# An attention scan and two mixtures of experts on one core: decay rows on ACT's DMA queue, two of eleven weight slots filled at the beginning, and another order of the last two attention steps, the tail and the preparation of w2

## The chip, the cores and the metric

The kernel runs on one core of a Trainium2 chip. The metric is the device time of one execution in microseconds (us), as the median of several runs. One further execution was recorded by the hardware profiler; all rows below come from it. The engines are named PE (TensorE matmul), PEld (its weight loads), DVE (VectorE), ACT (ScalarE), POOL (GpSimd) and SP (SyncE), and L352 is line 352 of the kernel.

## The reference

Three stages follow each other. The first is a gated linear attention over 4 batches, 8 heads, 768 positions and head size 40; the second a soft mixture of 8 experts with 4 slots each; the third a mixture whose weights are balanced over 8 rounds (Sinkhorn) and in which every expert sees all 3072 rows.

```python
# attention, per batch and head, t = 0..767
m_new  = max(f[t] + m, i[t])
C      = exp(f[t] + m - m_new) * C + exp(i[t] - m_new) * outer(v[t], k[t])
n      = exp(f[t] + m - m_new) * n + exp(i[t] - m_new) * k[t]
y[t]   = sigmoid(o[t]) * (C @ q[t]) / max(abs(n @ q[t]), 1)
# x: y as 3072 rows of 320
# first mixture (moe)
logits = x @ phi
d      = softmax(logits, over rows);   slot_in = d.T @ x
slot_out[e] = relu(slot_in[e] @ w1[e]) @ w2[e]
x      = softmax(logits, over slots) @ slot_out
# second mixture (moe2)
P = exp(x @ w_gate - max)
for _ in range(8): P /= P.sum(1) ; P /= P.sum(0) ; P *= N / E
out = sum over e of P[:, e] * (relu(x @ w1[e]) @ w2[e])
```

## The kernel before, in words

**Attention** is worked off in 24 tiles of 128 positions (all 8 heads of one batch, six tiles per batch). Keys and queries of a tile come in as kq (load_kq, L145, two loads of 160 KB made of 160-byte runs), values as vz (load_v, L150), the output gate as xr (load_o, L155). The gates are prepared once at the beginning (gates, L215 to L264): the running sum of the log decays is split into three bf16 parts, gp3, stored to DRAM as gpd (L250, L253), and read back per tile as three rows of the operand R (load_R, L308), the other 96 rows of which are a pattern of ones; its partner csl holds the input gates and is completed by small copies (load_csl, L275). One product of csl and R gives the exponents of a tile (e_p, L370, two halves per tile), ACT takes their exp into dd (L379), POOL cuts the triangle (L384), DVE multiplies in the scores q k (s_d, L407), and PE forms the value product from dd and vz (pv, L438); p_st (L448) adds the state of the earlier tiles. y_d (L459 to L476) and y_g (L486) normalise the tile into xr. x_p transposes finished tiles (L497), lg_p computes the logits (L520), lt_p, lt_d, lt_a and lt_f make the combine weights ct_all, and sl_p with sl_d (L592, L603) sum the dispatched rows into sacc.

**Order.** A step i of the loop mixes parts of several tiles; the string ORDER gives the sequence in which they are written, and PE, ACT and SP execute in that written order (manual schedules), while DVE and POOL are ordered by a scheduler. In step i, load_R fetches the decay rows of tile i + 3, needed by the exponent products of step i + 1; load_v fetches tile i + 2; load_kq tile i + 4; load_o tile i + 4; W fetches weights. All loads go over SP's queue. Ahead of the loop stands a prologue in which PE runs filler products (warm, WARM = [14, 10, 2, 2]).

**Weights.** The first mixture (MoE1) has 16 matrices of 1.28 MB, w1 and w2 of 8 experts. They go into slots (function slot): NRA = 9 slots exist while attention runs (wa, big, bigx, bigy) and are filled by parts, four per w1 and two per w2, WN[i] parts in step i; NRB = 6 further slots (wb) lie where attention's tiles were. Slot 14 takes w2 of MoE2's first expert, and freed slots are filled again.

**Tail.** After the loop, the string TAIL orders what is left: x22p, x22a, x23p, x23a are the transposes of the last two tiles and their copies; lp, ld, la, tp, tv and sp, sd the logits and the sums of the last group of four tiles; 0p to 4p with 0a and 0d transpose the combine weights of five of the six groups into cst (c_p, L787; c_a on ACT, L791; c_d on DVE, L795); ftp and ftd fold the sums into siT; wk is a pair of filler products (L872). Then MoE1 runs expert by expert (up, L910 and L917; up_t, L937; down, L948), the sixth group's c_p and the preparation of w2 of MoE2's first expert between them: amax takes the maxima, pow2_w a power-of-two scale, prep_a (ACT, L1023) and prep_d (DVE, L1027) split it into two f16 parts, wh and wl. Between MoE1 and MoE2 stand the fold of the slot outputs (L812), the router product (L1113), the first hidden weights of MoE2 (s1_p, s1_c) and the gate logits (gate_p, L1190).

**MoE2** takes 48 blocks of 512 rows: g1 (L1143) forms the hidden values z, ACT and DVE split them into hh and hl (L1146, L1147), and g2 multiplies them with wh and wl (L1164 to L1166).

Of the kernel before, what the change touches and what calls it, by code (L numbers as in the profile page):

```python
# [21 lines left out]
def mlstm_moe_kernel(  # L22
# [23 lines left out]
    P = 128  # L46
# [18 lines left out]
    ORDER = "LF' PK STm R DV DK O KT KTa ST STd E0 E0a E0g V I Y QT QTa Yg S W0 W1 E1 E1a E1g LP LV X Xa LD G LA W SM IR"  # L65
    PB = [1, 2, 3]
# [3 lines left out]
    NY = 2  # L70
    NRA = 2 + NBIG + NX + NY
    NRB = 6
# [105 lines left out]
    load_o(0, 1)  # L178

# [48 lines left out]
    def gates():  # L228
# [20 lines left out]

        nc.sync.dma_start(out=gpd[0:BH], in_=gp3[0:BH])  # L250
        load_R(0)
        load_R(1)
        nc.sync.dma_start(out=gpd[BH:GR], in_=gp3[BH:GR])  # L253
        load_kq(2)
        nc.scalar.copy(out=ident16, in_=ident)
        ids()
        init_R(0, 0, nc.scalar.copy)
        k_a(0, 0)
        k_a(0, 1)
        nc.scalar.activation(out=eG, in_=Gc, func=AF.Exp)  # L260
        nc.scalar.activation(out=eK, in_=eK, func=AF.Exp)
        for a, _ in zip((0, None, 1, None, 2), split3(cs3, bb, rk)):
            if a is not None:
                nc.gpsimd.tensor_copy(csl[a * BH:(a + 1) * BH, 0:SW], cs3[0:BH, a, :])  # L264
# [39 lines left out]
    def load_R(i):  # L304
# [3 lines left out]
        nc.sync.dma_start(out=t[96:99, :, :], in_=gpd[r0:r0 + H, :, o:o + L].rearrange("r a s -> a r s"))  # L308
# [318 lines left out]
    def slot(n):  # L627
# [10 lines left out]
        return rings["b"].tile([P, WSL], F32, tag="w", name="wb")  # L638
# [12 lines left out]
    def step(i):  # L651
# [6 lines left out]
        if gq < 0 or not X:  # L658
# [54 lines left out]
    load_v(1)  # L713
# [37 lines left out]
    WN = [0, 1, 1, 1] + [1 + (i % 6 > 3) for i in range(NT)]  # L751
# [3 lines left out]
    for i in range(NT + 1):  # L755
        step(i)
    if man2:
# [6 lines left out]
    rings["b"] = bctx.enter_context(tc.tile_pool(name="ring_b", bufs=NRB, side="right", reuse_waits="tile"))  # L764
# [3 lines left out]
    def load_n(n):  # L768

        if n < 2 * E - 2:  # L770
            load_w(m1_parts(n))
        elif n == 2 * E - 2:
# [26 lines left out]
    def c_m(g0, g1):  # L799
        nc.gpsimd.tensor_copy(cst[32:64, g0 * TB:g1 * TB], cst[0:32, g0 * TB:g1 * TB])  # L800
# [20 lines left out]
    cbk = [(ps_e, "e"), (ps_e, "e"), (ps_s, "s"), (ps_s, "s"), (ps_t, "t")]  # L821
# [52 lines left out]
    TAIL = "x22p x22a s4p wk 0p wk 1p x23p s4d 0a wk x23a lp wk 2p 1a 0d ld la mxp wk tp mxd ls lc 1d wk mbp mbd tv wk 3p mba fwd wk sp sd wk tq te wk ftp 4p ftd wk wk 2a 2d 3a 3d 4a ltd lta ltf 4d"  # L874
# [8 lines left out]
    for gq in range(gl):  # L883
# [11 lines left out]
    for gq in range(gl):  # L895
        c_m(gq, gq + 1)
# [45 lines left out]
    def down_p(e):  # L942
        hT = hTs.pop(e)
        w = m1[2 * e + 1].rearrange("p (k d) -> p k d", d=DM)
        pd = psy.tile([P, DM], F32, tag="y", name="pd")
# [96 lines left out]

    up(0)
    for e in range(E - 1):
        if e == 4:
# [8 lines left out]
        if e == 1:  # L1054
            c_p(gl, psp, "p")
            c_a(gl)
            c_d(gl)
            c_m(gl, NB)
        elif e == 4:
            src2[0] = w20[0].rearrange("p (k d) -> p k d", d=DM)  # L1060
# [293 lines left out]
```

## Time and profile before

| | us |
|---|---|
| median of 3 runs | 970.33 |
| lowest and highest run | 969.82 to 972.05 |
| the profiled execution, its own time | 971.88 |
| its span, first to last instruction | 969.6 |
| PE busy (7973 matmuls) | 939.5 |
| DVE busy | 569.1 |
| ACT busy | 357.3 |
| POOL busy | 88.2 |

The span is the time from the first to the last instruction of the profiled execution; its own time holds the launch around it too. A busy share is an average over stages that have different limits, and matmuls overlap in a pipeline, so PE's share says where PE was never idle rather than how fast it ran. Of 63.45 MB that DMA moved, most comes in the first 230 us: attention's inputs in short runs and the weights of MoE1.

### The profile page before, as it was taken

The numbers are of one execution on the slowest core, as the hardware profiler recorded it, in microseconds if no ns is written. First come the engines' busy times: TensorE is split into PE (matmuls) and PEld (weight loads), VectorE is DVE, ScalarE is ACT, GpSimd is POOL, SyncE is SP. The second block draws the span as 40 slices with busy tenths as digits, with TensorE's granted clock in tenths as the row PEclk, the third lists the DMA queues.
The fourth block names the chain that finished last, engine by engine and source line by source line (L and its number), as shares of the span: only waits on it lengthen the run. The fifth ranks groups of instructions, "written<-read, shape, count | busy, mean of one in ns | idle before, by whom it ended". The sixth has DMA issues, their size and how long they took to land.

```text
span 969.6 us, 18804 instructions
## 1 busy us (share of the span) xinstructions
PE 939.5 (97%) x7973; PEld 652.7 (67%) x7973; DVE 569.1 (59%) x1185; ACT 357.3 (37%) x696; POOL 88.2 (9%) x159
## 2 busy tenths in 40 slices
PE   6799999899999999999999999999999999999998
PEld 3687788535657766666666666666666666666665
DVE  6366466645778875474547456646755564554543
ACT  4254455334423334242434244224423342432321
POOL 4354344100000000000000000000000000000000
PEclk9799799999999999999999999999999999999999
DMA  6999999763020101010101011001100000000111
GB/s 95 159 179 191 183 192 233 266 213 120 15 85 12 40 15 55 1 55 1 55 1 55 1 55 28 30 1 55 55 1 1 1 1 1 1 2 28 48 41 48
DMA packets 129563, 63.45 MB, mean 65 GB/s; under 512 B 103528, under 2 KB 123272, under 8 KB 129480
## 3 DMA queue, kind: packets, MB, share of 16 engines
q1 hardware_dynamic: 129480, 62.26, 27.5%
q8 instruction: 62, 1.02, 0.5%
q14 instruction: 21, 0.17, 0.1%
HBM read 58.07 MB, written 4.08 MB: 64 GB/s over the span
## 4 chain that ended last, share of the span: by engine, by line
PE 93%; DVE 3%; ACT 1%; SPq 1%; DMA 1%; issue 1%; POOL 0%; DVEq 0%; ACTq 0%
PE y L1164 22%; PE y L1166 21%; PE y L1165 21%; PE z L1143 9%; PE oa L438 3%; PE ptk L352 2%; PE pss L400 2%; PE oa L448 2%; PE pu L910 2%; PE pe L370 2%; PE ob L412 1%; DMA R<-gpd 1%; PE pu L917 1%; PE pd L948 1%; PE ptx L497 1%; PE ob L285 1%
## 5 line engine op out<-in xcount | busy, mean ns | idle before, releaser
L1164 PE MATMUL y<-wx,hh 128*128 128x320 f16 x1344 | 403.8, 300 | 0.0
L1166 PE MATMUL y<-wx,hl 128*128 128x320 f16 x1344 | 401.9, 299 | 0.0
L1165 PE MATMUL y<-wx,hh 128*128 128x320 f16 x1344 | 401.9, 299 | 0.0
L1146 ACT ACTIVATE hh<-z 128x512 f16<-128x512 f32 x384 | 209.4, 594 | 452.4 <-PE z L1143 451.9
L1147 DVE SCALAR_TENSOR_TENSOR hl<-z,hh 128x512 f16<-128x512 f32 x384 | 248.3, 684 | 52.2 <-ACT hh L1146 51.6
L1179 DVE SCALAR_TENSOR_TENSOR acc<-y,Ps,acc 128x320 f32<-128x320 f32 x168 | 92.3, 549 | 218.3 <-PE y L1166 217.4
L1164 PEld LDWEIGHTS <-hh 128*128 128x128 f16 x1536 | 151.0, 98 | 100.8 <-issue 47.7
L1166 PEld LDWEIGHTS <-hl 128*128 128x128 f16 x1536 | 150.5, 98 | 61.1 <-DVE hl L1147 2.8
L1165 PEld LDWEIGHTS <-hh 128*128 128x128 f16 x1536 | 151.1, 98 | 51.4
L1143 PE MATMUL z<-cst,sst 96*128 96x512 f32 x384 | 142.0, 449 | 0.7 <-ACT gl L1198 0.4
L1143 PEld LDWEIGHTS z<-cst,sst 96*128 96x128 f32 x384 | 63.0, 191 | 11.1 <-issue 2.9
L1166 PE MATMUL y<-wh,hl 128*128 128x320 f16 x192 | 58.1, 303 | 0.8 <-DVE hl L1147 0.7
L1164 PE MATMUL y<-wh,hh 128*128 128x320 f16 x192 | 58.5, 304 | 0.0
L1165 PE MATMUL y<-wl,hh 128*128 128x320 f16 x192 | 58.1, 303 | 0.0
L360 ACT COPY T<-ptk 128x512 f32<-128x512 f32 x46 | 26.9, 586 | 41.5 <-PE ptk L352 41.5
L352 PE MATMUL ptk<-ident,kq 128*128 128x128 f32 x192 | 32.9, 301 | 8.5 <-POOL ident masks.py:199 8.5
L379 ACT ACTIVATE dd<-pe 128x512 f32<-128x512 f32 x48 | 29.0, 605 | 32.7 <-PE pe L370 31.8
L407 DVE TENSOR_TENSOR dd<-pss,dd 128x512 f32<-128x512 f32 x48 | 30.3, 671 | 7.1 <-PE pss L400 6.2
L459 DVE TENSOR_TENSOR u<-oa,eGt 128x164 f32<-128x164 f32 x20 | 6.6, 329 | 46.2 <-PE ob L448 46.2
L384 POOL TENSOR_SCALAR_AFFINE_SELECT dd<-dd 128x512 f32<-128x512 f32 x48 | 30.8, 641 | 25.9 <-ACT dd L379 25.4
L996 POOL PARTITION_ALL_REDUCE mr<-mxs x8 | 2.9, 368 | 309.8 <-DVE mxs L1015 309.8
L996 POOL PARTITION_ALL_REDUCE mr<-mx x8 | 3.0, 378 | 306.0 <-DVE mx L986 306.0
(230 smaller groups left out, 787.4 us busy)
## 6 DMA issues: line engine op xcount, KB each, us to landing
wa<-in_moe_w_dram SPq DMA_DIRECT2D x18, 512.0 KB, 6.0
raw<-in_moe_w_dram SPq DMA_DIRECT2D x28, 320.0 KB, 3.9
wb<-in_moe_w_dram SPq DMA_DIRECT2D x8, 640.0 KB, 7.8
kq<-in_k_dram SPq DMA_DIRECT2D x24, 160.0 KB, 4.9
kq<-in_q_dram SPq DMA_DIRECT2D x24, 160.0 KB, 5.2
vz<-in_v_dram SPq DMA_DIRECT2D x24, 160.0 KB, 4.3
xr<-in_o_gate_dram SPq DMA_DIRECT2D x24, 160.0 KB, 3.6
out_dram<-acc SPq DMA_DIRECT2D x24, 160.0 KB, 1.8
```

The costliest lines, as they stand in the source:

```text
L352: nc.tensor.transpose(pt[:, j, :], kq[i % NQ][:, a, 2 * j:2 * j + 2, :].rearrange("p h d -> p (h d)"), ident,)
L379: nc.scalar.activation(out=dd, in_=tmp.pop(("e", i, hh)), func=AF.Exp)
L384: nc.gpsimd.affine_select(out=dd, in_=dd, pattern=[[0, 4], [1, L]], compare_op=ALU.is_ge, fill=0.0, base=0, channel_multiplier=-1,)
L407: nc.vector.tensor_tensor(out=dds[i, r], in0=tmp["s", i][r], in1=dds[i, r], op=ALU.mult)
L438: nc.tensor.matmul(o_in[TH * a:TH * a + TH, 2 * j + r, :], dds[i, r][:, j, TH * a:TH * a + TH], vz[i % NV][:, 2 * j + r, :], start=True, s ...
L1143: nc.tensor.matmul(z, Sst[e][:, kc * P:(kc + 1) * P], cst[:, tb * TB:(tb + 1) * TB], start=True, stop=True,)
L1146: nc.scalar.activation(out=hh[:, kc, :], in_=z, func=AF.Relu)
L1147: nc.vector.scalar_tensor_tensor(out=hl[:, kc, :], in0=z, scalar=0.0, in1=hh[:, kc, :], op0=ALU.max, op1=ALU.subtract)
L1164: nc.tensor.matmul(y, hh[:, kc, ts], wh[e][:, kc, :], start=(kc == 0), stop=False)
L1165: nc.tensor.matmul(y, hh[:, kc, ts], wl[e][:, kc, :], start=False, stop=False)
L1166: nc.tensor.matmul(y, hl[:, kc, ts], wh[e][:, kc, :], start=False, stop=(kc == KF - 1))
L1179: nc.vector.scalar_tensor_tensor(out=a, in0=y, scalar=Ps[:, i, e:e + 1], in1=a, op0=ALU.mult, op1=ALU.add)
```

## The change

The change moves the stores of gpd, the loads of R and the copies of csl from SP's queue to ACT's; loads tile 2 of kq early; loads the first two weight matrices (one expert) in the prologue and gives bigy four slots instead of two and wb four instead of six, each with a name of its own; spreads the other weight parts one per step (WN), more in the last steps; orders DVE by hand in the last three steps, with another sequence (ORDER_L); writes the tail in another order, with three c_p in it instead of five and three wk instead of twelve; puts the other three c_p behind the first three experts; starts the maxima of w2 after experts 1 and 2 and converts one quarter after each of the experts 3 to 6; copies the combine rows (c_m) with one load on ACT's queue instead of six copies on POOL; computes s1_p ahead of the router product; and adds filler products (warm2) at the end of MoE1 and at the gate.

```diff
+    ORDER_L = "LF' PK STm R DV DK O ST STd V I S W0 W1 Y Yg LP LV X Xa LD G LA W"
-    NY = 2
+    NY = 4
-    NRB = 6
+    NRB = 4
     load_o(0, 1)
+    load_kq(2)
...
-        nc.sync.dma_start(out=gpd[0:BH], in_=gp3[0:BH])
-        load_R(0)
-        load_R(1)
-        nc.sync.dma_start(out=gpd[BH:GR], in_=gp3[BH:GR])
-        load_kq(2)
         nc.scalar.copy(out=ident16, in_=ident)
         ids()
         init_R(0, 0, nc.scalar.copy)
+        nc.scalar.dma_start(out=gpd[0:BH], in_=gp3[0:BH])
         k_a(0, 0)
-        k_a(0, 1)
         nc.scalar.activation(out=eG, in_=Gc, func=AF.Exp)
         nc.scalar.activation(out=eK, in_=eK, func=AF.Exp)
+        k_a(0, 1)
+        load_R(0)
+        load_R(1)
+        nc.scalar.dma_start(out=gpd[BH:GR], in_=gp3[BH:GR])
...
     def load_csl(g_):
-            nc.sync.dma_start(
+            nc.scalar.dma_start(
-    WARM = [14, 10, 2, 2]
+    WARM = [14, 3, 2, 2]
     def load_R(i):
-        nc.sync.dma_start(out=t[96:99, :, :], ...)
+        nc.scalar.dma_start(out=t[96:99, :, :], ...)
...
-            DV=lambda: T and load_v(n),
+            DV=lambda: T and i and load_v(n),
-        for o in ORDER.split():
+        for o in (ORDER if i < NT - 2 else ORDER_L).split():
...
-    load_v(1)
...
+    load_w(islice(ahead_parts, 2))
+    load_v(1)
+    load_v(2)
+    load_w(islice(ahead_parts, 2))
     load_o(1, O0)
+    load_w(islice(ahead_parts, 2))
     load_kq(3)
     load_csl(2)
-    load_w(islice(ahead_parts, 2))
...
-    WN = [0, 1, 1, 1] + [1 + (i % 6 > 3) for i in range(NT)]
+    WN = [0] + [1] * 19 + [2, 2, 2, 3, 0]
-    for i in range(NT + 1):
+    for i in range(NT - 2):
         step(i)
+    man2d = tc.manual_schedule(engines={mybir.EngineType.DVE})
+    man2d.__enter__()
+    for i in range(NT - 2, NT + 1):
+        step(i)
+    man2d.__exit__(None, None, None)
...
-    def c_m(g0, g1):
-        nc.gpsimd.tensor_copy(cst[32:64, g0 * TB:g1 * TB], cst[0:32, g0 * TB:g1 * TB])
+    def c_m():
+        nc.scalar.dma_start(out=cst[32:64, :].bitcast(F32), in_=cst[0:32, :].bitcast(F32))
-    cbk = [(ps_e, "e"), (ps_e, "e"), (ps_s, "s"), (ps_s, "s"), (ps_t, "t")]
+    cbk = [(ps_e, "e"), (ps_s, "s"), (ps_s, "s")]
-    TAIL = "x22p x22a s4p wk 0p wk 1p x23p s4d 0a wk x23a lp wk 2p 1a 0d ld la mxp wk tp mxd ls lc 1d wk mbp mbd tv wk 3p mba fwd wk sp sd wk tq te wk ftp 4p ftd wk wk 2a 2d 3a 3d 4a ltd lta ltf 4d"
+    TAIL = "x22p x22a 0p s4p 0a x23p x23a s4d 1p 2p lp 1a wk ld la mxp ls tp mxd wk tv mbp 0d mbd mba sp lc fwd sd wk tq ftp 1d te ftd 2a ltd lta ltf 2d"
...
     for e in range(E - 1):
-        if e == 4:
+        if e == 3:
             man4 = tc.manual_schedule(...)
...
-        if e == 1:
-            c_p(gl, psp, "p")
-            c_a(gl)
-            c_d(gl)
-            c_m(gl, NB)
-        elif e == 4:
-            for kk in range(4):
-                amax(0, kk)
-        elif e > 4:
-            if e == 5:
+        if e < 3:
+            c_p(3 + e, psp, "p")
+            c_a(3 + e)
+            c_d(3 + e)
+            if e:
+                for kk in range(2 * e - 2, 2 * e):
+                    amax(0, kk)
+        else:
+            if e == 3:
+                c_m()
                 pow2_w(0)
-            for kk in range(2 * e - 10, 2 * e - 8):
-                prep_a(0, kk)
-                prep_d(0, kk)
+            prep_a(0, e - 3)
+            prep_d(0, e - 3)
+    def warm2(n):
+        pw2 = psz.tile([P, TB], F32, tag="z", name="pw2").rearrange("p (a l) -> p a l", a=4)
+        for _ in range(n):
+            nc.tensor.matmul(pw2, ident16, ident16.unsqueeze(1).to_broadcast([P, 4, L]), start=True, stop=True)
     up_t(E - 1)
+    warm2(2)
     down_p(E - 1)
     down_d(E - 1)
+    warm2(4)
     fold_t(pt, soa, fold)
+    warm2(2)
+    s1_p(0)
+    pow2_s(0)
...
     gate_p(1)
+    s1_c(0, 0, True)
     gate_a(0)
-    s1_c(0, 0, True)
     gate_t(0)
+    warm2(2)
```

Three places show how the order changes. The first is SP's queue in the prologue, from the load of v of tile 1 on (wa are MoE1's first slots, kq_104 receives tile 3). Before:

```order
L150 DMA vz_111<-in_v_dram 128x8x40
L155 DMA xr<-in_o_gate_dram 128x8x40 x2
L145 DMA kq_104<-in_k_dram 128x8x40
L145 DMA kq_104<-in_q_dram 128x8x40
L275 DMA csl<-gbuf 32x256 x3
L622 DMA wa<-in_moe_w_dram 128x1024 x2
L155 DMA xr<-in_o_gate_dram 128x8x40 x2
L308 DMA R_122<-gpd 3x8x128
```

With the change, from the load of tile 2 on:

```order
L146 DMA kq_106<-in_k_dram 128x8x40
L146 DMA kq_106<-in_q_dram 128x8x40
L623 DMA wa<-in_moe_w_dram 128x1024 x2
L151 DMA vz_111<-in_v_dram 128x8x40
L151 DMA vz_112<-in_v_dram 128x8x40
L623 DMA wa<-in_moe_w_dram 64x512 x2
L156 DMA xr<-in_o_gate_dram 128x8x40 x2
L623 DMA wa<-in_moe_w_dram 128x4x320 x2
L146 DMA kq_104<-in_k_dram 128x8x40
L146 DMA kq_104<-in_q_dram 128x8x40
```

The loads of R and csl are gone from SP, six parts of the first two weight matrices stand ahead of the keys of tile 3, and v of tiles 1 and 2 comes early.

The second is ACT's queue with the change, from the end of the prologue into step 1, each row with what it waits for (DMAHW0 to DMAHW7 are eight counters that the DMAs take in turn; T are the copies of transposed keys and queries). Before, the same rows stood there without the two loads:

```order
L165 ACTIVATE xr<-xr 128x2x320 [waits DMAHW0_49]
L309 DMA R_122<-gpd 3x8x128 [waits DMAHW1_49]
L361 COPY T_349<-ptk 128x512 [waits PE_49,Activation_49]
L380 ACTIVATE dd<-pe 128x512 [waits PE_49]
L361 COPY T_391<-ptk 128x512 [waits PE_49]
L380 ACTIVATE dd<-pe 128x512 [waits PE_49]
L309 DMA R_121<-gpd 3x8x128 [waits DMAHW6_49]
L361 COPY T_424<-ptk 128x512 [waits DVE_49,PE_49]
```

R of tile 3 is issued ahead of step 0's first copy and R of tile 4 ahead of step 1's, each behind a wait for a counter.

The third is PE at the beginning of the tail (ptx are transposes of tiles, ptc those of the combine weights, pq is sl_p, pl the logits). The rows left out are the filler pairs. Before:

```order
L497 MATMUL ptx<-ident,xr 112x128 x6
L592 MATMUL pq<-xr,lt 32x321 x4
...
L787 MATMUL ptc<-ident,ct_all 32x128 x4
...
L787 MATMUL ptc<-ident,ct_all 32x128 x4
L497 MATMUL ptx<-ident,xr 112x128 x3
...
L520 MATMUL pl<-xT,phi_sb 32x128 x12
```

With the change:

```order
L498 MATMUL ptx<-ident,xr 112x128 x6
L796 MATMUL ptc<-ident,ct_all 32x128 x4
L593 MATMUL pq<-xr,lt 32x321 x4
L498 MATMUL ptx<-ident,xr 112x128 x3
L796 MATMUL ptc<-ident,ct_all 32x128 x8
L521 MATMUL pl<-xT,phi_sb 32x128 x12
```

The second c_p has moved from ahead of the last tile's transposes to behind them, two of them now stand between those and the logits, and no filler does.

## Rows read from the trace of the kernel before

**Rows 1.** The page: busy time, share of the span and instructions of each engine
```profile
PE 939.5 (97%) x7973; PEld 652.7 (67%) x7973; DVE 569.1 (59%) x1185; ACT 357.3 (37%) x696; POOL 88.2 (9%) x159
```

**Rows 2.** Windows: busy us (instructions) by engine, granted clock, DMA share, GB/s
```profile
18.00:20.00 2.00, 1.31 (x12) 0.62 (x11) 0.00 (x0) 1.01 (x2) 0.80 (x2) 1.00 0.00 0
28.00:34.00 6.00, 1.05 (x19) 0.65 (x17) 1.12 (x3) 0.84 (x2) 1.26 (x3) 0.98 1.09 233
34.00:43.00 9.00, 9.00 (x86) 7.52 (x85) 3.29 (x9) 2.50 (x5) 2.72 (x4) 0.50 1.06 115
96.00:100.00 4.00, 1.81 (x22) 1.14 (x21) 0.37 (x2) 2.53 (x7) 0.23 (x2) 0.82 1.00 259
100.00:108.00 8.00, 8.00 (x67) 7.09 (x66) 3.65 (x11) 1.76 (x4) 2.67 (x4) 0.50 1.15 190
222.00:225.00 3.00, 3.00 (x26) 1.09 (x19) 0.54 (x2) 0.00 (x0) 0.00 (x0) 0.52 1.07 395
```

**Rows 3.** Chain that ended last, in order: start us, length us, engine, tile
```profile
29.07 4.59 DMA R<-gpd
...
34.32 1.87 PE oa L438 x32
...
44.06 1.06 PE oa L438 x32
...
60.74 1.06 PE oa L438 x32
...
66.51 1.06 PE oa L438 x32
...
93.08 5.51 DMA R<-gpd
...
99.25 1.87 PE oa L438 x32
...
109.58 1.06 PE oa L438 x32
...
172.99 1.33 PE oa L438 x32
```

**Rows 4.** Timeline of SP's queue: start us, us, line, DMA, count
```profile
25.72 2.15 SPq L622 DMA_DIRECT2D wa<-in_moe_w_dram  x2
27.91 1.06 SPq L155 DMA_DIRECT2D xr<-in_o_gate_dram  x2
29.07 2.00 SPq L308 DMA_DIRECT2D R<-gpd  x1
...
91.83 1.21 SPq L622 DMA_DIRECT2D big<-in_moe_w_dram  x2
```

**Rows 5.** Timeline of the opening: the second group of fillers on PE
```profile
15.95 2.32 PE L285 MATMUL ob<-ident 128*128 128x512 f16 x10
```

**Rows 6.** Tile R: issues of its loads, ns minimum/median/maximum, first and last start
```profile
L308 SPq DMA_DIRECT2D R<-gpd x24: 244/328/1999, 11.7 to 156.9; - x24
```

**Rows 7.** Timeline of POOL at the second hole, with idle time before
```profile
92.69 0.72 POOL L343 TENSOR_TENSOR kp<-kq,eKt 128x320 f32<-128x320 f32 x1 [0.66 <-DMA kq<-in_k_dram]
```

**Rows 8.** Timeline of the tail, DVE and PE, with idle time before
```profile
178.35 0.48 DVE L486 TENSOR_TENSOR xr<-xr,nq 128x320 f32<-128x320 f32 x1
...
180.31 0.61 PE L787 MATMUL ptc<-ident,ct_all 128*32 128x128 f32 x4 [1.87 <-DVE cst L795]
...
180.76 0.49 PE L497 MATMUL ptx<-ident,xr 128*112 128x128 f32 x3
...
189.68 0.26 DVE L862 TENSOR_TENSOR siT<-ob,rs 128x96 f32<-128x96 f32 x1
...
190.35 1.07 PE L910 MATMUL pu<-wa,siT 128*32 128x256 f32 x16
```

**Rows 9.** Timeline of MoE1's end and of MoE2's first products on PE
```profile
215.63 1.28 PE L948 MATMUL pd<-wb,hT 128*32 128x320 f32 x16 [1.78 <-ACT hT L939]
...
227.42 0.70 PE L1143 MATMUL z<-cst,sst 96*128 96x512 f32 x2 [0.30 <-DVE sst L1095]
```

More of the change, by code (lines that the diff above doesn't have):

```diff
@@ L307, in load_R @@
         t = Rt[(b % 2) * 2 + c % 2]
-        nc.sync.dma_start(out=t[96:99, :, :], in_=gpd[r0:r0 + H, :, o:o + L].rearrange("r a s -> a r s"))
+        nc.scalar.dma_start(out=t[96:99, :, :], in_=gpd[r0:r0 + H, :, o:o + L].rearrange("r a s -> a r s"))
     def decays_d():
@@ L637, in slot @@
             return bigy[n - NRA + NY]
-        return rings["b"].tile([P, WSL], F32, tag="w", name="wb")
+        return rings["b"].tile([P, WSL], F32, tag=f"w{n - NRA}", name=f"wb{n - NRA}")
     def m1_parts(n, place=None):
@@ L763, in mlstm_moe_kernel @@
     pb = bctx.enter_context(tc.tile_pool(name="pb", bufs=2, side="right", reuse_waits="tile"))
-    rings["b"] = bctx.enter_context(tc.tile_pool(name="ring_b", bufs=NRB, side="right", reuse_waits="tile"))
+    rings["b"] = bctx.enter_context(tc.tile_pool(name="ring_b", bufs=1, side="right", reuse_waits="tile"))
     m2w, w20 = {}, {}
     def load_n(n):
-        if n < 2 * E - 2:
+        if n < NRA:
             load_w(m1_parts(n))
-        elif n == 2 * E - 2:
+        elif n == NRA:
             w20[0] = slot(n)
@@ L882, in mlstm_moe_kernel @@
     )
-    for gq in range(gl):
+    for gq in range(len(cbk)):
         ops[f"{gq}p"] = lambda gq=gq: c_p(gq, *cbk[gq])
@@ L894, in mlstm_moe_kernel @@
         man3.__exit__(None, None, None)
-    for gq in range(gl):
-        c_m(gq, gq + 1)
     actx.close()
@@ L944, in down_p @@
         w = m1[2 * e + 1].rearrange("p (k d) -> p k d", d=DM)
-        pd = psy.tile([P, DM], F32, tag="y", name="pd")
+        pd = psy.tile([P, TB], F32, tag="y", name="pd")[:, 0:DM]
         for t in range(2):
@@ L1041, in scale_p @@
         )
+    sgs = sm_p.tile([CK, 7 * NS], F32R, name="sgs")
+    for c0, c1 in ((0, P), (P, 7 * NS)):
+        nc.vector.tensor_scalar_mul(sgs[:, c0:c1], ones[0:CK, 0:c1 - c0], 0.0)
+    sg = sgs[:, 3 * NS:3 * NS + E]
+    src2[0] = w20[0].rearrange("p (k d) -> p k d", d=DM)
     up(0)
     for e in range(E - 1):
-        if e == 4:
+        if e == 3:
             man4 = tc.manual_schedule(engines={mybir.EngineType.Activation, mybir.EngineType.DVE, mybir.EngineType.Pool})
@@ L1108, in s1 @@
             s1_c(e, j, True)
-    pg8 = psy.tile([P, DM], F32, tag="y", name="pg8")
+    s1_p(0)
+    pow2_s(0)
+    pg8 = psy.tile([P, TB], F32, tag="y", name="pg8")[:, 0:DM]
     for kt, (o, n) in enumerate(KS):
@@ L1119, in mlstm_moe_kernel @@
     nc.vector.tensor_tensor(out=sg[32:64], in0=pg8[0:NS, 0:E], in1=sg[0:32], op=ALU.subtract)
-    s1_p(0)
-    pow2_s(0)
     bctx.close()
@@ L1160, in g2 @@
         if k0 == 0:
-            y0[tt] = psy.tile([P, DM], F32, tag="y", name="y")
+            y0[tt] = psy.tile([P, TB], F32, tag="y", name="y")[:, 0:DM]
         y = y0[tt]
@@ L1187, in gate_p @@
         b0, n = gates2[gg]
-        tmp["ga", gg] = psz.tile([P, TB], F32, tag="z", name="pgl")
+        tmp["ga", gg] = psy.tile([P, TB], F32, tag="y", name="pgl")
         for j in range(n):
```

5 lines of the change are left out of this document (removed).

## The prediction

> **What bounds the kernel now.** I read the page first, then PE's busy time by windows, then the chain that ended last, then the single instructions at the places where PE stood still. PE is busy 97% of the 969.6 us span; ACT is busy 37% [rows 1]. From its first product at 227.42 us [rows 9], the second mixture (MoE2) runs in an order that the change leaves alone, so whatever can be won lies ahead of it, in holes of PE and in stretches where the granted clock is 0.50, that is 1.2 of its two levels 1.2 and 2.4 GHz.
>
> The first hole is in the opening. In the window from 28 to 34 us PE is busy 1.05 of 6.00 us: 4.95 idle [rows 2]. The chain names the decay rows of tile 3 (R, loaded by load_R) as what ended it: 4.59 us from 29.07 [rows 3]. SP reached that load only at 29.07, after two halves of a weight matrix (2.15 us) and two o_gate tiles (1.06), and took 2.00 us to issue it [rows 4]. After the hole the granted clock is 0.50 from 34 to 43 us [rows 2]: the value product (pv) of the next step takes 1.87 us instead of 1.06, and from that product to the next one is 9.74 us (34.32 to 44.06), where an undisturbed step takes 5.77 (60.74 to 66.51) [rows 3].
>
> The second hole has the same cause. At 93.08 the chain waits 5.51 us for a load of R [rows 3], which SP issued behind two weight parts [rows 4]; PE is busy 1.81 of 4.00 us from 96 to 100, 2.19 idle, with 0.50 granted from 100 to 108 [rows 2], and the step behind it lasts 10.33 us (99.25 to 109.58) instead of 5.77 [rows 3]. So each hole costs its idle time and nearly twice that in clock.
>
> **The opening.** The two stores of the gate rows (gpd), the six copies of csl and all 24 loads of R leave SP's queue for ACT's; SP gets the third key/query tile, the whole first expert of MoE1 (six weight parts) and v of tiles 1 and 2 before it first has to wait for compute. R of tile 3 is then issued by ACT ahead of its first copy of step 0, a whole step before PE wants it. Idle time won: 4.95. The slow step behind it: 9.74 - 5.77 = 3.97. Seven of the ten filler matmuls at 15.95 go; ten take 2.32 [rows 5], seven 1.62, and they stand directly ahead of the first exponent product on PE, so that comes earlier. Against it three small copies now stand on ACT ahead of the first exponentials; I take 0.3 off: 1.3. Together 10.2.
>
> What an issue costs on ACT, the trace of before does not show: ACT issues none. On SP the issue of R takes 0.24 us at least, 0.33 in the middle and 2.00 at most [rows 6]. A queue of its own could cost ACT nothing, or, where it must wait, more than 2.00. I take 0.33, the middle, because ACT's queue carries only small loads. 24 loads are 8 us of ACT in 170; PE, not ACT, sets the length of a step, so I cost them at nothing. Their cover is the time for which ACT waits for PE in each step; if that went, each step would grow by 0.33, 8 us in all. At 2.00 each it would be 48 us of ACT, and the cover would hardly hold: the ground of rival (d).
>
> **The middle.** With R off SP's queue the stall at 96 has no cause of its own left: 2.19 idle and 10.33 - 5.77 = 4.56 of clock, 6.75 together. What is late next is the key tile: at 92.69 POOL waits 0.66 us for one [rows 7], so SP's lag was nearly the limit for keys too. In the steps up to there SP has less to carry than before: one weight part a step instead of up to two, since six parts were loaded at the beginning, and no R.
>
> One rule speaks against this. The row shows 5.51 us from the start of R's issue to its landing, with its own bytes being 6 KB: nearly all of it is spent behind other loads [rows 3]. The Trainium skill (DMA: Bandwidth & Descriptors, section "Issuing engines are not separate DMA queues") says that loads started by different engines run on the same DMA engines and interleave, so that another issuing engine saves only the time to start them. By that rule the bytes ahead of PE's need stay the bound, the middle would not be won, and the sum would be 21.3 - 6.75 = 14.55 us: rival (a) below. I go by the rows all the same: ACT comes to the load at the start of step 10, before the key tile's use at 92.69 [rows 7], while PE wants R in step 11 (96 us); even 5.51 us behind other loads it lands in time.
>
> **The end of attention.** In the last two steps DVE runs by a written order: first the two score products that PE waits for, then y of tile 22, then y of tile 23 without foreign work in it. In the tail the transposes of the combine weights (c_p) use other PSUM buffers, three instead of five stand there, and nine of twelve pairs of filler matmuls (wk) go. Before, the last tile is ready at 178.83 (178.35 + 0.48), but PE waits 1.87 us at 180.31 for the buffer of a c_p that stands ahead of it and starts the tile's transposes at 180.76 [rows 8]: 1.9 us late. That goes; on DVE y of tile 23 starts no earlier than before, since the order puts 1.3 us of score products ahead. Between the transposes and siT (189.68 + 0.26) lie 9.2 us [rows 8]; on PE five filler pairs between them go, 10 x 0.232 = 2.3 us [rows 5], of which I put 1.35 on the path, because the rest waits for DVE and ACT. Last, up(0) started 0.41 after siT (190.35), behind a c_p and two wk [rows 8]; now nothing stands there. Sum 3.65. Bounds: 1.5, if DVE's new order delays the logits of group 4 and only the buffer wait is won, and 5, if all filler was on the path.
>
> **MoE1 and the gate.** At 215.63 PE waits 1.78 us for ACT, which does two conversions of w2 ahead of the copy that PE needs [rows 9]; the change does one conversion per expert and starts one expert earlier: -1.78. Two more c_p come here from the tail, 0.61 each [rows 8]: +1.2. The first conversion now waits for its scale while hT of the next expert stands behind it on ACT: 0 to 0.6, I take 0.3. At the gate 0.52 is granted from 222 to 225 [rows 2]; ten fillers keep it busy there, and s1_p comes before the router product. But the first z at 227.42 [rows 9] also needs the scale from DVE and the gate's copy on ACT, which are not shorter. I take 0.4 (0 to 1.5). Both stages together 0.7. The copy of the combine rows goes from POOL to one load on ACT; it has four experts' time to land and I cost it at nothing; if it were late, the gate products would wait for it.
>
> **Sum.** 10.2 + 6.75 + 3.65 + 0.7 = 21.3 us. The profiled execution took 971.88, so 950.6; it stands 1.55 above the median of 970.33, against which the runs of the change will be read: **949.0 us**. If all goes as drawn, single terms err by some 3.5 us either way: 945.5 to 952.5.
>
> **Rivals.**
> (a) Bytes, not the queue, bound the middle. For it: the late key tile [rows 7]: 0.66 us then, and more if PE comes there over ten us sooner while the bytes do not. Against: fewer weight bytes a step until step 10, and keys are asked for two steps ahead. The wait of 2.19 and the clock behind it come back: 949.0 + 6.75 = 955.8.
> (b) The weights ahead of keys make the opening wait in another place. For it: six parts now stand before the keys of tile 3 on SP. Against: from 18 to 20 us DMA moves nothing at all [rows 2]. A wait of 3 us with 4 of clock: 956.
> (c) With nine filler pairs gone, the clock falls in the tail or in MoE1. For it: the holes above that ended in half clock were 2.2 and 4.95 us. Against: the 1.87 us one did not. Four to ten us at half clock cost 2 to 5: 952.5.
> (d) Slower: ACT itself gets stuck. In the program's listing a load of R on ACT waits for a DMA counter that an SP load two steps back uses, so a late SP stops ACT in front of the copies, exponentials and everything that PE needs of it. It decides the sign from 21.3 us in 22 steps, that is if PE loses over 0.97 us per step; at 1.5 us it gives 949.0 + 33 = 982. For it: SP's lag [rows 4, 7]. Against: the counter's load is one whose data the same step needs anyway.
> (e) The loads of R are issued earlier but other waits keep PE where it was, within noise: 970.
>
> **How the numbers follow.** Forecast 0.67, (a) 0.13, (b) 0.07, (c) 0.07, (d) 0.04, (e) 0.02. A measurement of this kernel tells some 0.2% (1.9 us) from no change. Faster is the forecast with (a), (b) and (c): 0.94; same is (e): 0.02; slower is (d): 0.04. The range reaches from the lower end of the forecast's own range, 945.5, past (a), (b) and (c) to 958; some 0.14 is left out.
>
> **What would show it.** Right: PE busy without a hole from 28 to 34 and from 96 to 100 us; pv of steps 1 and 11 at 1.06; the granted clock at full from 20 to 180 us; the last pv at about 156 instead of 172.99 [rows 3]; the gap from there to up(0) some 14 us instead of 17.4 (190.35 - 172.99). Rival (a) shows as PE or POOL waiting for kq or vz, (b) as the same before 40 us, (c) as a clock of 0.50 between 156 and 205, (d) as PE waiting for ACT's T or dd while ACT waits for a DMA. The forecast is wrong if MoE2's first product starts later than 215 us (it should at 227.42 - 21.3 = 206).

## The result, and the profile after

The changed kernel takes 956.79 us (median of 4 runs, 953.80 to 960.78), the kernel before 971.19 beside it: a ratio of 0.985 (95% interval 0.9803 to 0.9896). Measured again with five runs beside later experiments it takes 954.52 against 969.84, 0.9847 (0.9823 to 0.9871). So it is faster by 14.4 and 15.3 us, where 21.3 were forecast; the forecast of 949.0 is missed by 7.8 and 5.5 us, the range of 945.5 to 958 holds both medians. Executions of either kernel differ by up to 7 us, along with the mean granted clock: of the changed kernel's first four, the two with a mean of 0.994 and 0.995 took 955.48 and 953.80, the two with 0.988 and 0.989 took 960.78 and 958.09. The profiled one is that of 958.09, with a span of 956.4 us, 13.2 less than before.

The page of the changed kernel, where [rows 1] had PE at 939.5 us:

```profile
PE 932.8 (98%) x7958; PEld 648.7 (68%) x7958; DVE 569.7 (60%) x1185; ACT 357.5 (37%) x696; POOL 84.2 (9%) x153
```

Windows of the changed kernel (engines, granted clock, DMA share and GB/s as in [rows 2]):

```profile
16.00:20.00 4.00, 2.14 (x15) 1.17 (x13) 2.17 (x8) 1.14 (x3) 1.49 (x3) 1.00 1.17 195
21.00:35.00 14.00, 14.00 (x116) 10.46 (x112) 6.13 (x14) 5.27 (x10) 6.26 (x12) 0.52 1.01 184
92.00:100.00 8.00, 8.00 (x140) 6.58 (x129) 5.29 (x18) 5.47 (x15) 4.38 (x8) 1.00 0.94 159
100.00:108.00 8.00, 8.00 (x129) 6.21 (x127) 4.59 (x14) 4.13 (x9) 4.11 (x8) 1.00 1.25 235
...
212.00:216.00 4.00, 3.79 (x13) 2.14 (x12) 0.75 (x2) 2.54 (x5) 0.39 (x1) 0.58 0.01 4
```

Where [rows 2] had the second hole, from 92 to 108 us, PE is now never idle and the clock is full. But a stretch that used to be full, 21 to 35 us, now runs at 0.52: the clock fell there after a window from 16 to 20 in which PE is busy 2.14 of 4.00 us. At the gate it falls too (212 to 216), as it did before.

I read the time off PE's timeline at five marks that both kernels have: the third value product (pv), that of step 22, the first up, the fold of the slot outputs (pt_so) and the first z. Lengths in us:

| stretch | before | after | gained | forecast |
|---|---|---|---|---|
| start to third pv | 43.99 | 40.95 | 3.04 | 10.2 |
| third pv to pv of step 22 | 124.33 | 117.26 | 7.07 | 6.75 |
| pv of step 22 to up(0) | 22.03 | 18.37 | 3.66 | 3.65 |
| up(0) to pt_so | 29.54 | 29.57 | -0.03 | 0.3 |
| pt_so to first z | 7.53 | 7.92 | -0.39 | 0.4 |
| first z (227.42, now 214.07) to the end | 742.18 | 742.33 | -0.15 | 0 |

The gains sum to 13.2. Of the 8.1 us that are missing, 7.2 lie ahead of the third pv. PE's timeline of the changed kernel there (start, length, instructions; in brackets PE's idle time and what ended it):

```profile
16.86 0.81 PE L286 MATMUL ob<-ident 128*128 128x512 f16 x3
18.01 0.38 PE L371 MATMUL pe<-R,csl 99*128 99x512 bf16 x1 [0.35 <-DMA R<-gpd]
19.90 0.38 PE L371 MATMUL pe<-R,csl 99*128 99x512 bf16 x1 [1.51 <-ACT dd L380]
...
27.86 1.94 PE L439 MATMUL oa<-vz,dd 128*64 128x41 f32 x32
...
35.51 1.13 PE L439 MATMUL oa<-vz,dd 128*64 128x41 f32 x32
```

Before:

```profile
18.11 0.38 PE L370 MATMUL pe<-R,csl 99*128 99x512 bf16 x1
19.18 0.38 PE L370 MATMUL pe<-R,csl 99*128 99x512 bf16 x1 [0.69 <-ACT dd L379]
```

The first exponent product waits 0.35 us for R of tile 0, the second 1.51 us for ACT, where it had waited 0.69 before. ACT and SP of the changed kernel in the same stretch (the ...q rows are DMA issues), and then the store of gpd and the first loads of R before:

```profile
9.81 0.38 ACTq L255 DMA_DIRECT2D gpd<-gbuf  x1
...
14.38 0.77 ACTq L309 DMA_DIRECT2D R<-gpd  x2
...
16.68 0.54 ACTq L276 DMA_DIRECT2D csl<-gbuf  x1
...
18.05 1.16 ACTq L276 DMA_DIRECT2D csl<-gbuf  x2
19.25 0.60 ACT L380 ACTIVATE dd<-pe 128x512 f32<-128x512 f32 x1 [2.09 <-DVE gbuf L315]
```

```profile
9.23 1.29 SPq L623 DMA_DIRECT2D wa<-in_moe_w_dram  x2
10.72 1.59 SPq L151 DMA_DIRECT2D vz<-in_v_dram  x2
12.77 3.26 SPq L623 DMA_DIRECT2D wa<-in_moe_w_dram  x2
...
18.42 2.31 SPq L623 DMA_DIRECT2D wa<-in_moe_w_dram  x2
```

```profile
10.14 0.33 SPq L250 DMA_DIRECT2D gpd<-gbuf  x1
11.70 0.62 SPq L308 DMA_DIRECT2D R<-gpd  x2
```

ACT stores gpd at 9.81 and issues R only at 14.38, 4.6 us later; before it was 1.56 (10.14 to 11.70 on SP), with a DMA share of 0.12. Now SP has the keys of tile 2, four weight parts and v of tiles 1 and 2 out by then, and R lands at 18.0. Behind that ACT issues two csl copies (18.05, 1.16 us) and starts the first exponential at 19.25; before it started at 18.53.

The tail, MoE1 and the gate on PE, beside [rows 8] and [rows 9]:

```profile
163.82 1.13 PE L439 MATMUL oa<-vz,dd 128*64 128x41 f32 x32 [1.18 <-DVE u L467]
...
168.79 0.51 PE L498 MATMUL ptx<-ident,xr 128*112 128x128 f32 x3 [0.66 <-DVE xr L487]
...
176.58 1.07 PE L917 MATMUL pu<-wa,siT 128*32 128x256 f32 x16 [0.97 <-DVE siT L871]
...
179.29 0.41 PE L944 MATMUL pth<-ident,h 128*128 128x128 f32 x2 [1.07 <-DVE cst L804]
...
195.59 1.28 PE L955 MATMUL pd<-bigy,hT 128*32 128x320 f32 x16 [0.55 <-ACT hT L946]
...
206.15 0.53 PE L821 MATMUL pt_so<-fold,soa 128*128 128x32 f32 x4
...
210.79 1.66 PE L1204 MATMUL pgl<-cst,sgs 96*128 96x512 f32 x6 [1.40 <-DVE sgs L1135]
...
214.07 1.84 PE L1157 MATMUL z<-cst,sst 96*128 96x512 f32 x3
```

### The profile page after: what moved, and what is told of

Same layout as the page of the kernel before. It is cut to its first block, busy times and chain, and to the rows that moved or that the text cites. A ratio compares the mean times of both kernels' runs of the same rounds, so it can differ in the third digit from the quotient of the medians.

```text
span 956.4 us, 18788 instructions
## 1 busy us (share of the span) xinstructions
PE 932.8 (98%) x7958; PEld 648.7 (68%) x7958; DVE 569.7 (60%) x1185; ACT 357.5 (37%) x696; POOL 84.2 (9%) x153
## 4 chain that ended last, share of the span: by engine, by line
PE 93%; issue 3%; DVE 3%; ACT 1%; POOL 0%; POOLq 0%; DVEq 0%; ACTq 0%
PE y L1178 22%; PE y L1180 22%; PE y L1179 22%; PE z L1157 9%; PE ptk L353 3%; PE pss L401 3%; PE oa L439 3%; PE oa L449 2%; PE pe L371 2%; PE ob L413 1%; PE ptx L498 1%; PE pu L917 1%; PE ob L286 1%; PE pu L924 0%; DVE mx L993 0%
## 5 line engine op out<-in xcount | busy, mean ns | idle before, releaser
L353 PEld LDWEIGHTS ptk<-ident,kq 128*128 128x128 f32 x192 | 23.5, 152 | 10.3 <-POOL ident masks.py:199 8.9
```

The source lines that it names most:

```text
L353: nc.tensor.transpose(pt[:, j, :], kq[i % NQ][:, a, 2 * j:2 * j + 2, :].rearrange("p h d -> p (h d)"), ident,)
```

## The experiments

Theories for the opening: A, the clock falls because seven fillers are gone; B, csl on ACT holds the first exponential; C, weight bytes hold R. Rivals for the middle: R's place in SP's queue, or the uneven weights (two parts in some steps). Each run left one profile; waits and marks are read from it, times and ratios from all executions. All diffs are against the changed kernel unless said otherwise; each was timed in five rounds beside the kernel before.

**Ten fillers again.**

```diff
-    WARM = [14, 3, 2, 2]
+    WARM = [14, 10, 2, 2]
```

> The changed kernel with ten fillers again in place of three ahead of the first exponent products. In the changed kernel's profile PE idles 0.34 us at 17.67 and 1.51 us at 18.39, and the granted clock is 0.50 from 21.3 to 35 us. Theory A (the seven missing fillers): PE stays busy to the first exponent products, the clock stays full, the 4.8 us of half clock (2.55 in step 0, 2.2 in step 1) come back: 951.5 us. Theory B (two issues of csl copies on ACT ahead of the first exponential) and theory C (weight bytes that make the decay rows land late): the hole ahead of the second product stays over 1 us, the clock falls all the same: 956 to 957.5.

Median 953.58 (951.46 to 961.18), ratio 0.9839 (0.9812 to 0.9866). The profiled execution is the longest of the six: third pv at 41.82, half clock from about 21 to 34.

```profile
19.04 0.38 PE L371 MATMUL pe<-R,csl 99*128 99x512 bf16 x1 [0.59 <-DMA R<-gpd]
20.92 0.59 PE L371 MATMUL pe<-R,csl 99*128 99x512 bf16 x1 [1.51 <-ACT dd L380]
```

PE still waits 0.59 for R and 1.51 for ACT, and the clock falls all the same: A is not the whole cause. It may be a part: four of the six executions have a mean clock of 0.996 or more, which none of the nine of the changed kernel reaches (0.988 to 0.995). By the medians it can't be told, the intervals overlap.

**csl behind the first exponentials.**

```diff
-    load_csl(1)
...
     load_R(2)
+    load_csl(1)
```

> The changed kernel with the three csl copies of the prologue issued on ACT behind the first two exponentials and the next load of R in place of ahead of them. Theory B: the first exponential starts at 18.6 instead of 19.25, the hole behind the first exponent product shrinks from 1.51 to about 0.7 as before the change, the clock stays full: 950.5 to 951.5. Theory A: the hole shrinks but the clock falls all the same: 955.5 to 956.5. If the exponential waits for the masks on DVE and not for ACT's queue, nothing moves: 956.8.

957.29 (955.26 to 957.85), 0.9863 (0.9849 to 0.9877). Third pv at 37.66.

```profile
18.91 0.59 PE L371 MATMUL pe<-R,csl 99*128 99x512 bf16 x1 [3.10 <-DMA R<-gpd]
20.18 0.59 PE L371 MATMUL pe<-R,csl 99*128 99x512 bf16 x1 [0.68 <-ACT dd L380]
```

The second product's wait fell from 1.51 to 0.68: csl on ACT did make that hole, B holds for it. But R of tile 0 lands at 18.9, PE waits 3.10 for it, and the clock falls. With ten fillers as well, the run below, PE comes to the first product without a wait for R, and then waits 2.8 us for csl of tiles 2 and 3, which was issued at 20.77 instead of 16.68:

> Both the ten fillers and the late csl copies. If A or B alone restores the clock, this adds at most 0.8 us to the better one: 950 to 951. If each alone leaves the clock at half and the fall needs both, this is the first at full clock: 950.5, against 956 for the two alone. Under C alone: 956.

```profile
PE pe L371 <- DMA csl<-gbuf: 2.8, 1, 2.8
```

958.92 (957.12 to 959.78): a miss, 8 us over what was expected.

**Two weight parts in the prologue instead of six.**

```diff
-    load_w(islice(ahead_parts, 2))
     load_v(1)
     load_v(2)
-    load_w(islice(ahead_parts, 2))
     load_o(1, O0)
-    load_w(islice(ahead_parts, 2))
     load_kq(3)
     load_csl(2)
+    load_w(islice(ahead_parts, 2))
...
-    WN = [0] + [1] * 19 + [2, 2, 2, 3, 0]
+    WN = [0] + [1] * 15 + [2] * 4 + [2, 2, 2, 3, 0]
```

> The changed kernel with two weight parts in the prologue, behind the keys of tile 3, in place of six ahead of them; the four others are loaded in steps 16 to 19. Theory C: gpd's store and R land some 3 us earlier, the first exponent product is bound by PE alone at about 17.5, the hole shrinks and the clock stays full: 950 to 951. Theories A and B: R is earlier, but the hole behind the first product and the half clock stay: 955.5 to 957.

953.59 (952.64 to 957.65), 0.9831 (0.9812 to 0.9849).

```profile
10.63 0.37 ACTq L255 DMA_DIRECT2D gpd<-gbuf  x1
...
14.05 0.77 ACTq L309 DMA_DIRECT2D R<-gpd  x2
```

```profile
16.79 0.38 PE L371 MATMUL pe<-R,csl 99*128 99x512 bf16 x1
18.45 0.38 PE L371 MATMUL pe<-R,csl 99*128 99x512 bf16 x1 [1.28 <-ACT dd L380]
```

```profile
PE ob L413 <- DMA vz<-in_v_dram: 2.1, 1, 2.1
```

R no longer holds PE, in this execution the clock stays full in the opening although a hole of 1.28 behind the first product is there, and the third pv comes at 34.50: 9.5 of the 10.2 us are won. C holds by this profile; by the times the run is not told apart from the changed kernel, the intervals overlap. But the weights are not all that makes R late. From gpd's store to the issue of R it still takes 3.4 us here; in the five profiles with no weight issued before 16.7 us it takes 3.4 to 4.0, in the seven with the changed order of the loads 3.4 to 5.7, and before it took 1.56. Under way at that time in all twelve are the other loads that the change moves ahead, keys of tile 2 and v of tiles 1 and 2; they were not tried alone. The weights show in the whole way from the store to the first exponent product: 8.2 to 8.7 us where PE waits for R behind them, at most 6.2 to 7.0 without them. The four late parts then cost some of it: a wait of 2.1 for v at 153.57, two stretches at half clock behind it, and 1.3 us more from step 22 to up(0).

**The changed kernel again**, unchanged:

> The changed kernel as it is, on the chip of this call, beside the next three. Theory (the clock's fall in the opening comes in some executions and not in others, since its holes of 0.35 and 1.51 us lie at the edge): the executions fall into two groups, near 953.5 us with a mean granted clock of 0.994 or more, and 956.5 to 961 with 0.991 or less. If the fall is fixed by the program, all lie within 2 us.

954.52 (954.05 to 956.27), all five clocks between 0.992 and 0.995: no second group, the expectation was wrong there. Its profile is still the best evidence on the clock:

```profile
17.93 0.38 PE L371 MATMUL pe<-R,csl 99*128 99x512 bf16 x1 [1.26 <-DMA R<-gpd]
19.82 0.59 PE L371 MATMUL pe<-R,csl 99*128 99x512 bf16 x1 [1.51 <-ACT dd L380]
```

```profile
20.00:21.00 1.00, 1.00 (x7) 0.67 (x8) 0.00 (x0) 0.56 (x1) 0.49 (x1) 0.50 0.80 188
...
23.00:24.00 1.00, 0.93 (x4) 0.29 (x3) 1.00 (x3) 0.47 (x1) 0.00 (x0) 0.98 0.99 352
```

The holes are no smaller than in the first profile (1.26 and 1.51 against 0.35 and 1.51), and the second product starts within 0.1 us of the same time. But here the granted clock is back at 23 us, there at 35; the third pv comes at 36.55 instead of 40.95. A third profile of the same opening, that of the gate's edit below, has holes of 1.46 and 1.66, half clock for some 3.5 us and the third pv at 37.56.

**R alone on ACT's queue**, against the kernel before:

```diff
-        nc.sync.dma_start(out=t[96:99, :, :], ...)
+        (nc.scalar if i >= 2 else nc.sync).dma_start(out=t[96:99, :, :], ...)
```

> The kernel before with one part of the change alone: the loads of R from tile 2 on are issued by ACT; fillers, weights and all else as before. If SP's queue alone caused both holes: no wait for R, PE full from 28 to 34 us and from 90 to 108, gain 8.9 (4.95 idle and 3.97 clock) and 6.75, 15.6 together: 955.3. If the bytes of two weight parts a step bound the middle (rival a): the opening's 8.9 alone, 962, with a wait for kq, vz or R near step 11.

962.40 (961.19 to 966.30), 0.9928 (0.9905 to 0.9950): what rival (a) expected. The third pv comes at 33.78, a gain of 10.21, but the stretch to step 22 takes 127.52 instead of 124.33. PE's waits by cause (us in total, times, longest):

```profile
PE ptk L352 <- DMA kq<-in_k_dram: 3.7, 3, 1.8
...
PE ptk L352 <- ACT xr L164: 2.1, 2, 1.2
```

The wait for R is gone and one for key tiles has taken its place, with half clock from about 135 to 141; another 2.1 us the profile puts down to ACT's xr, a tile that these products do not read, so what held them stays open. The stretch also begins 10.21 us earlier here, so that its loads are wanted sooner: of that lead 7.02 is left at the pv of step 22 (161.30 against 168.32).

**R back on SP, with the change's weights:**

```diff
-        nc.scalar.dma_start(out=t[96:99, :, :], ...)
+        (nc.sync if i >= 3 else nc.scalar).dma_start(out=t[96:99, :, :], ...)
```

> The changed kernel with one part undone: the loads of R of tiles 3 to 23 stand on SP's queue again, the weights spread as in the change (six parts in the prologue, one a step). If R's place in SP's queue made the middle hole whatever the weights do: a wait for R of 2 us or more near step 11 and half clock behind it, 961 to 963; in the opening a wait for R of tile 3. If the even spread of the weights alone freed the middle: no wait there, 954 to 957.

957.80 (955.63 to 963.31), 0.988 (0.9852 to 0.9909). The stretch to step 22 takes 119.04, with no hole near step 11:

```profile
PE pe L371 <- DMA R<-gpd: 2.5, 5, 1.0
```

So of the middle's 7.07 us the change without R's new queue brings 5.3 (124.33 - 119.04). What acts in these steps is the placing of the weights, six parts ahead and then one a step; the even spread was not tried by itself. R's queue adds 1.0 to 1.8 to it (119.04 against 117.26, 117.54 and 118.07 in three profiles with the changed kernel's attention); alone, above, it makes the stretch 3.2 longer. By the times this run is not told apart from the changed kernel.

**Another order of the loads on SP.** First all six csl copies on SP, ahead of the six weight parts; then csl of the second segment, four parts, the keys of tile 3, csl of the third segment, two parts (in place of the prologue's order):

```diff
-            nc.scalar.dma_start(
+            nc.sync.dma_start(
                 out=csl[a * BH:(a + 1) * BH, g_ * SW:(g_ + 1) * SW], ...
...
+    load_v(1)
+    load_v(2)
+    load_o(1, O0)
     load_csl(1)
...
-    load_w(islice(ahead_parts, 2))
...
+    load_w(islice(ahead_parts, 4))
     load_kq(3)
     load_csl(2)
+    load_w(islice(ahead_parts, 2))
```

> The changed kernel with the six csl copies on SP's queue again, ahead of the six weight parts, which thereby leave SP only when csl's source is ready, behind the issue of R of tiles 0 and 1. If weight bytes made R land late and csl's issues on ACT held the first exponential: first exponent product at about 16.8, the second at 17.9 to 18.4 with a hole of 0.7, third pv at 33.5 to 34.5 instead of 40.95 us, the clock at full in the opening: 950.5. If neither was the cause: third pv at 39 to 41, 956.

> As the run with all csl copies on SP, but with another order on SP: the csl copies of the second segment, four weight parts, the keys of tile 3, the csl copies of the third segment, the other two weight parts. Theory (what the opening lost is the order of the loads: weights ahead of R of tile 0, or ahead of the keys of tile 3): no wait of over 1 us for R, csl or kq before 40 us, third pv at 33.5 to 34.5 us, last pv at 156.5 to 158 instead of 159.7 to 163.8, the clock at full in the opening: 949.5 to 951.5. Rival (the weight bytes have to cost the opening something wherever they stand): a wait of 2 us or more comes back in steps 1 to 3, with the clock: 955 or more.

The first took 960.04 (957.48 to 960.25), 0.9895 (0.9874 to 0.9915), the second 959.18 (956.97 to 961.43), 0.9889 (0.9866 to 0.9913): neither is faster than the changed kernel, the first is slower. In the first the opening begins as expected (products at 16.62 and 17.68), then stands still for key tile 3:

```profile
13.61 4.75 SPq L276 DMA_DIRECT2D csl<-gbuf  x6
18.41 3.45 SPq L623 DMA_DIRECT2D wa<-in_moe_w_dram  x6
...
24.24 1.29 SPq L146 DMA_DIRECT2D kq<-in_q_dram  x1
```

```profile
30.76 1.09 PE L353 MATMUL ptk<-ident,kq 128*128 128x128 f32 x4 [4.53 <-DMA kq<-in_k_dram]
```

The csl copies hold SP for 4.75 us, the weights follow, and the keys' second load (24.24) comes behind all of them. That is rival (b) as it was drawn, the keys of tile 3 behind the weights. In the second run it is the third segment's csl that holds SP, 4.74 us from 20.39; the clock falls from about 25 to 31, and the third pv comes at 37.59. The bytes cost the opening something in every order tried here with six parts.

**The gate's old order.**

```diff
-    s1_p(0)
-    pow2_s(0)
-
     pg8 = ...
...
     nc.vector.tensor_tensor(out=sg[32:64], ...)
+    s1_p(0)
+    pow2_s(0)
...
-    s1_c(0, 0, True)
     gate_a(0)
+    s1_c(0, 0, True)
```

> The changed kernel with one part undone: at the gate the router product and its copies stand again ahead of the hidden product of MoE2 (s1_p) and its scale, and gate_a ahead of s1_c. Theory (the gate got slower because DVE's part of the router copy stands behind the scale chain, 1.40 us of wait at 210.79): the wait goes, from the fold of the slot outputs to the first z it takes 6.6 to 7 us instead of 7.92: 955.5. Rival (the scale chain is the longer one, which the change started earlier): the first z comes 0.5 us later, 957.3.

952.71 (950.82 to 956.83), 0.9828 (0.9802 to 0.9854).

```profile
203.57 0.53 PE L821 MATMUL pt_so<-fold,soa 128*128 128x32 f32 x4
...
206.75 1.65 PE L1203 MATMUL pgl<-cst,sgs 96*128 96x512 f32 x6
...
209.57 0.71 PE L1156 MATMUL z<-cst,sst 96*128 96x512 f32 x2
```

From pt_so to the first z it takes 6.00 instead of 7.92 (8.22 in the changed kernel's second profile), without a wait for sgs; by the times the run is not told apart from the changed kernel. The clock has a part in it: it stays full here, and falls at the gate in all nine profiles with the changed order. The gate of the kernel before, this order without fillers, took 7.53 with the clock down at 222; in the run with R alone on ACT, the same instructions and the same waits ahead of them, it took 5.99 at full clock:

```profile
212.86:218.85 5.99, 5.13 (x48) 3.12 (x49) 1.78 (x7) 1.76 (x6) 0.37 (x1) 1.00 1.06 376
```

So the old order is worth 1.9 against the changed one, but against the kernel before only as much as the clock gives back, and at full clock the fillers make the stretch no shorter. With the second order of loads above, the same edit gives 5.99:

> The same order on SP, and the gate's old order (router product and its copies ahead of the hidden product and its scale, gate_a ahead of s1_c). If both gains are independent: another 1.8 to 2 us, 947.5 to 949.5, under both kernels. If the gate's gain was one of the clock in that execution alone: as the run before.

That run took 958.79 (956.83 to 960.12), 0.9883 (0.9859 to 0.9907): the gate's gain is there, but in its profile PE waits 3.9 us for a key tile and the clock is at half for some 10 us behind that, and its median stays above the changed kernel's.

**Two weight parts, the rest after the last key tiles, and the gate's old order:** the prologue of the third diff, the gate's diff, and

```diff
-    WN = [0] + [1] * 19 + [2, 2, 2, 3, 0]
+    WN = [0] + [1] * 19 + [2, 2, 2, 7, 0]
```

> The changed kernel with two weight parts in the prologue, behind the keys of tile 3, in place of six (as in the third run), the four parts that are left over loaded at the end of step 23 instead of in steps 16 to 19, and the gate's old order. Theory (the opening's loss is the weights ahead of R, the late loss of the third run was v behind two parts a step, the gate's loss is DVE's place behind the scale chain; all independent): third pv at 34 to 35 us, no wait for vz in steps 20 to 23, last pv at 157 to 158.5, first z 6 us behind the fold of the slot outputs: 949 to 951, under the run with the gate alone. Rival (MoE1 then waits for the late weights): a wait of up for DMA after 176 us, 952 or more.

951.69 (949.46 to 953.95), ratio 0.9807 (0.9788 to 0.9826): the lowest ratio of all, under both kernels; its interval touches that of the changed kernel at 0.9823 to 0.9826 and overlaps that of the gate's edit alone, so against that one it is not told apart. Its profile shows the stretches as expected but for the last pv:

```profile
core 0: 947.7 us, clock 1.000
```

```profile
20.00:36.00 16.00, 15.40 (x247) 12.37 (x244) 9.67 (x25) 8.34 (x16) 10.42 (x19) 1.00 1.10 191
```

Third pv at 33.93, last at 159.01 (0.5 us past the expected range, behind three waits for R of 2.3 together), pt_so to first z 6.01, first z at 207.33, the clock full in the opening and at the gate in this execution (the mean clock of the other four is 0.994 to 0.998). No wait for the weights appears in MoE1. The profiled execution took 949.46, where the forecast for the change stood at 949.0.

## Why the prediction was right or wrong

Of the signs that I had named, both holes are gone (PE is busy throughout from 28 to 34 and from 92 to 108), and the clock is full behind 35 us up to the gate, but not from 21 to 35, where full clock was forecast. The last pv comes at 163.82 where 156 was named, and up(0) 12.8 behind it instead of 14. The first z comes at 214.07, between the 206 that was forecast and the 215 above which the forecast was to count as wrong. That the time lies in the range is no merit of the sum of 949: the range was drawn past the rivals' prices. The remark that a hole costs nearly twice its idle time in clock holds for the second hole (2.19 and 4.56), not for the first (4.95 and 3.97); the sum used the right terms.

**The opening (10.2 forecast, 3.04 in the profile, 7.44 and 6.43 in two others of the same opening): wrong, and it is the step that failed.** The old cause was read rightly: with R's loads moved alone, the third pv came 10.21 us earlier. What failed is what the change adds there. I let "the third key/query tile, the whole first expert of MoE1 (six weight parts) and v of tiles 1 and 2" go ahead and costed them at nothing, and put the fillers on the path ("that comes earlier", 1.3 us). In fact R of tile 0 is stored and read back through DRAM while these loads are under way, and PE waits for it, with three fillers (0.35 and 1.26 in the two profiles) and with ten (0.59). So the fewer fillers won nothing. The three csl copies for which I took 0.3 us off hold ACT's queue for 1.70 us (0.54 and 1.16), the last two of them in front of the first exponential, and the second product's wait grows from 0.69 to 1.51. So the first exponent product comes at 18.01 instead of 18.11 and the second at 19.90, 0.72 later than before (19.18). Behind these holes the granted clock falls: in the first profile for 14 us. Between the two profiles of the changed kernel that length is worth 4.4 us (40.95 against 36.55); the other 2.6 (36.55 against 33.93) go with four of the six parts out of the way. Why the clock stays down for 14 us in one execution and for some 3.5 in another of the same program, no run shows. Rival (b) named the weights, at 0.07, but had the keys of tile 3 wait for them, not R; that its price of 956 is close to the 956.79 is chance. I held against it that DMA moved nothing from 18 to 20 us; that idle time was there before the change, which filled it (share 1.17 from 16 to 20).

**The middle (6.75 forecast, 7.07): the size right, the reason only in part.** I took SP's queue as the cause. The two experiments show 5.3 us with R still on SP and the weights placed as in the change, and 3.2 lost in this stretch with R alone on ACT (127.52 us against 124.33), the wait moved to the keys. The Trainium skill (DMA: Bandwidth & Descriptors, section "Issuing engines are not separate DMA queues") has the rule that I set aside: loads issued by different engines run on the same DMA engines, so that another issuer saves only the time to start them. The run with R alone on ACT agrees with it. What I held against rival (a), fewer weight bytes a step, is the larger part of the gain.

**The tail (3.65 forecast, 3.66): right, with two terms left out of the sum, which cancel.** By DVE's timeline the last tile is ready at 168.65 and siT at 176.53. The tile's transposes start 0.14 later (168.79), where they were 1.93 late: 1.79 for 1.9. From them to siT 7.74 instead of 9.18: 1.44 for 1.35. From siT to up(0) 0.05 instead of 0.41. The tile itself is ready 10.44 after the pv of step 22 instead of 10.51, and these sum to 3.66. What I had left out: the last pv waits 1.18 us for DVE's u (the row at 163.82), where DVE's new order has both score products and a part of y in front, and comes 5.61 instead of 4.67 behind that of step 22. Against that DVE does y of tile 23 in 2.64 instead of 3.46, with no foreign work in it, and starts it 2.19 instead of 2.38 behind that pv. So the last tile is no later, but the new order of DVE wins next to nothing (0.07) up to there. Of rival (c) the changed kernel's two profiles show nothing, but three of the experiments, in code that they share with it, do: half clock for some 7 us between 174 and 185, and 31.8 us instead of 29.57 from up(0) to pt_so, 2.3 of the 2 to 5 that (c) was priced at.

**MoE1 (0.3 forecast, -0.03).** The stall of 1.78 us for hT is 0.55 now, as expected. New is a wait of 1.07 for DVE at 179.29: on DVE the last c_d of the tail stands behind the softmax of the sixth group. The c_p cost 0.45 each, less than 0.61.

**The gate (0.4 forecast, -0.39): the sign was wrong.** I saw that the first z needs the scale and the gate's copy, but not that DVE's part of the router copy would now stand behind the scale's chain: PE waits 1.40 at 210.79, and behind that the clock falls as before. Undone, the gate takes 6.00 at full clock, no less than the kernel before's at full clock (5.99): what there was to win here was the clock (7.53 - 5.99), and the fillers did not keep it with the changed order.

**R on ACT (nothing forecast):** right. An issue took 0.24 us (24 of them, 0.485 at most), less than the 0.33 I assumed, and no wait of PE in the changed kernel goes back to it. Rival (d) did not come; where R moves alone, the profile puts 2.1 us of PE's waits down to ACT, with the doubt named above.

## What to carry to other kernels

Before loads are moved into an idle stretch of DMA, look at what makes a round trip through DRAM there: here the read of a small store could be issued 1.56 us behind it with DMA nearly idle and 3.4 to 5.7 with large loads out, and what waits for it waits at the head of the program. When a queue seems to be the bound, move one load off it alone and see whether the wait only changes its name; here the placing of the weights did most of what the other queue was credited with. Before a stretch is called faster by its order, compare the granted clock in it: the same gate took 7.53 and 5.99 us. An order that starts one chain earlier has to be read on every engine for what it puts behind that chain.

## What the runs showed of the hardware

- The same program, behind the same hole of 1.51 us, ran at half clock for 14 us in one profiled execution and for some 3.5 in another; with two weight parts, behind 1.28 and 1.17 us, the clock did not fall in either profile. Behind the one wait of 2.4 us in MoE2 (Sinkhorn's sums) it fell in twelve of fourteen profiles and not in those of the two kernels with the best medians, where the first z to the end takes 740.4 us instead of 742. At the gate of the kernel before, behind the same waits, it fell in one profile (7.53 us) and not in another (5.99).
- gpd's store to the issue of its first read: 1.56 us with a DMA share of 0.12; 3.4 to 4.0 in five profiles with keys and v out, 3.4 to 5.7 in seven with weights out as well.
- A csl copy (32 x 256 bf16, from SBUF to SBUF) held its issuing engine for 0.51 to 0.98 us, and once each for 2.4 and 2.5, R's load of 3 x 8 x 128 on ACT for 0.24 in the middle; six csl copies in a row held SP for 4.75.
